# Two more token pairs in the half form of the state space stage

## The chip, the cores and the metric

The kernel runs on one core of one Trainium2 chip. Its time is the device time of one execution in microseconds (us). The core has five engines that work side by side, each through its own list of instructions in order: TensorE (PE in the profile, with its weight loads as PEld), VectorE (DVE), ScalarE (ACT), GpSimd (POOL) and SyncE (SP), which here only issues transfers (DMAs). They wait for each other by semaphores.

## The reference

A state space layer is followed by a two-layer network. Per batch, head and chunk the first one computes, with L the decay between two positions and `state` carried from chunk to chunk:

```
CB = einsum('bhin,bhjn->bhij', Cc, Bc);  M = CB * L
y  = einsum('bhij,bhjd->bhid', M, xc) + einsum('bhin,bhnd->bhid', Cc, state) * decay_to_i
state = decay_full * state + sum_j Bc * xc * decay_from_j
h = x @ w_in;  g = max(h, 0) + alpha * min(h, 0);  out = g @ w_out
```

There are 4 batches, 8 heads, 768 positions, 32 values per head and 16 state rows; the result, 3072 tokens of 256 values, goes through w_in (256 x 2048) and w_out (2048 x 256). All is float32. The chunk in the kernel is 128 positions (the result does not depend on it).

## The kernel before

**Tokens.** The 3072 tokens are 24 chunks of 128, worked in 12 pairs (0 to 11) of two chunks; a batch has 3 pairs, so pairs 2, 5, 8 and 11 end one. Two pairs fill one block of 512 tokens, of which the network handles one at a time; there are 6 blocks.

**First block.** `first_two` handles pairs 0 and 1. The loop over `f` (16 slices of the hidden layer) then runs the network on block 0 by `hidden(0, f)` (two products into a PSUM tile `hp`, then the activation on ScalarE, L1098, and on VectorE, L1099) and `output(f - 4)`, and among them the conversion of the weights (`convert_a`, `convert_b`: L273 and L286 on ScalarE, L278 and L330 on GpSimd, L296 and L308 on VectorE), pairs 2 and 3, and the loads of pairs 3 and 4 (`load_pair`, at f = 5 and 10). There are two `hp` tiles, so a product into one waits until VectorE has read what was in it before. At f = 14 VectorE also runs the scans over the rows of `a` of batches 2 and 3 (L437 to L483), and GpSimd makes `bn` (B times the decay to the end, `pair_loads`, L533) for pair 4.

**Later blocks.** `quad(g, z, after, third)` is a quarter of the hidden layer for block g: products `first` (L1241) into `ss` and `hp` tiles, the activations (`prelu`, L1224 and L1226), and sums of results on GpSimd (L1288, L1298). Its calls `after(j)` place everything else by hand: `product` (L1216), the last `output` steps of block 0 (L1142), weight sums on GpSimd (`weight_sums`, L1171) and the steps of the pairs (table `steps`). The second product of a quad, into `Y` with weights `s1`, takes the token sum `t1` that GpSimd makes in `token_sums` (L1183); `Y` of the first quad is the `hp` tile of `hidden(0, 15)`.

**A pair** (`pair(gp)`, a generator): `added` makes the state update (L629), `states` applies it (L642), `sm` masks the state on GpSimd (L645), B and C are turned so that positions lie along the free axis, `scan_half` makes the decays on VectorE from rows loaded in `abc`, `spread_c` and `c_decayed` make `cz` (ScalarE, L679) and `cd` (GpSimd, L682), `products_bc` makes C·B into `gram` tiles (two `ss`, two `hp`), VectorE multiplies them with the decays (L753), and the products with x and with the state give `y` (L797 and L805), which ScalarE copies to `xT`.

**Full and half form.** Pairs 2 to 5 use the full form: products over 128 positions and scans of 256 columns (L567). Pairs 6 to 11 (`gp >= HALF`) use the half form: the two halves of a chunk of 128 positions are handled as 64 each, on the two halves of the partitions, so that the part of the 128x128 square above the diagonal that is zero is not computed. The decay rows are 192 columns (`SQ`) rather than 256 (scans at L561), the products are L618, L731, L779 and L787, and two copies each of `cd` (ScalarE, L690) and of the state (GpSimd, L692) move them to the other half of the partitions (`moved`). The loads are 64 partitions at a time (L146, L154), 17 DMAs for a pair.

**Turning.** Pairs 5 to 11 load B and C so that VectorE turns them in one instruction (`turn_bc`, L574), with the first two decay scans behind it; pairs 2 to 4 are turned by TensorE (four transposes, L669) and a copy on ScalarE (L672).

**Constants.** `m5_bank` is a PSUM bank whose right half holds the identity that the scans read; `halve_identity` rewrites its lower partitions for the half form. `scratch["z", i]` are the decay rows in DRAM, from which `abc` is loaded; `prt` holds the decays to the end, turned by `rows_turn`.

Of the kernel before, what the change touches and what calls it, by code (L numbers as in the profile page):

```python
# [9 lines left out]
F32 = mybir.dt.float32  # L10
# [12 lines left out]
def kernel(  # L23
# [25 lines left out]
    nc = tc.nc  # L49
# [4 lines left out]
    batch, H, S, D = x.shape  # L54
# [22 lines left out]
    WQ = 256  # L77
    HQ = Q // 2
    SQ = Q + HQ
    HALF = NP // 2  # L80
    assert H * N == P and HD == d_model and KC == 2 and R == CPB == 6
    assert NCH % GC == 0 and GT == 512 and NF % 8 == 0 and d_model <= WQ

# [65 lines left out]
    def load_spread(gp, b, c):  # L149

        for w, t in enumerate(loads["p", gp][1] if gp >= HALF else ()):
            rows = scratch["z", b // 2].rearrange("(b h c) t -> b c h t", b=2, h=H)
            for k in range(2):
                nc.sync.dma_start(  # L154
                    out=t[HQ * k : HQ * (k + 1), : 4 * SQ].rearrange("p (h t) -> p h t", h=4),
                    in_=rows[b % 2, c + k, 4 * w : 4 * w + 4].unsqueeze(0)
                    .to_broadcast([HQ, 4, SQ]))
        for k, t in enumerate(loads["p", gp][1] if gp < HALF else ()):
            rows = scratch["z", b // 2].rearrange("(b h c) t -> b c h t", b=2, h=H)[b % 2, c + k]
            nc.sync.dma_start(out=t.rearrange("p (h t) -> p h t", h=H),  # L160
                              in_=rows.unsqueeze(0).to_broadcast([P, H, Q]))
            yield
# [7 lines left out]
    def load_pair(gp, decays=True, parted=False):  # L170


        b, c = divmod(2 * gp, CPB)
        turned = gp > GC
        nat = ldx.tile([P, 3, 2, H * N], F32, name="nat")
        xt = ldx.tile([P, 2, HD], F32, name="xt")

        ap = ldx.tile([P, 2 * Q], F32, name="ap")
        if gp == 0:
            load_a(ap, b, c)  # L180
        elif gp > NB:
            load_products(gp, ap)
        if gp == 0:
            load_rows(0, nc.scalar)
        abc = []
        if gp >= HALF:
            load_tokens(nat[:, 0], B[b], c * Q)
        def load_bc(k):
            ts = slice((c + k) * Q, (c + k + 1) * Q)
            for i, src in enumerate((B,) if turned else (B, C)):  # L190
                eng = nc.scalar if gp == 0 and i else nc.sync
                eng.dma_start(out=nat[:, i, k].rearrange("p (h n) -> p h n", h=H),  # L192
                              in_=src[b, :, ts, :].rearrange("h p n -> p h n"))

        def load_x(k):
            ts = slice((c + k) * Q, (c + k + 1) * Q)
            nc.sync.dma_start(out=xt[:, k].rearrange("p (h d) -> p h d", h=H),  # L197
                              in_=x[b, :, ts, :].rearrange("h p d -> p h d"))

        for k in range((1 if parted else 2) if gp < HALF else 0):  # L200
            load_bc(k)
            if gp >= NB:
                load_x(k)
        for k in range(2 if gp < NB else 0):
            load_x(k)
        if gp == 0:
            nc.scalar.dma_start(out=al_n, in_=moe_alpha.rearrange("(k p) -> k p", p=P))
            loads["a", 1] = prep.tile([P, 2 * Q], F32, name="a1")
            load_a(loads["a", 1], b, c + 2)
        for i, src in enumerate((B, C) if turned else ()):  # L210


            for e in range(2):
                first = src[b, e : e + 1, c * Q : (c + 2) * Q, :]
                nc.sync.dma_start(out=nat[:, 1 + e, i],
                                  in_=bass.AP(tensor=first.tensor, offset=first.offset,
                                              ap=[[2 * S * N, P // 32], [8 * N, 32], [1, 8 * N]]))
        for k in range(2 if gp >= NB else 0):
            abc.append(lda.tile([P, H * Q], F32, name="abc"))
        loads["p", gp] = nat, abc, xt, ap  # L220
        if gp >= HALF:
            load_tokens(xt, x[b], c * Q)
        if decays:
            for part in load_spread(gp, b, c):
                pass
        return lambda: load_bc(1), lambda: load_x(1)
# [193 lines left out]

    def halve_identity():

        for s in range(2):
            nc.scalar.copy(
                out=ident_p[0][HQ:].rearrange("p (a s t) -> p s a t", a=2, s=2)[:, s],
                in_=ident[HQ:, HQ * (1 - s) : HQ * (2 - s)].unsqueeze(1).to_broadcast([HQ, 2, HQ]))
# [45 lines left out]
    def rows_out(i):  # L472


        if i == 0:
            scratch["z", 0] = dr.tile([RW, Q], F32, name="z0")
            nc.sync.dma_start(out=scratch["z", 0], in_=held.pop("z"))
            return
        d0 = held.pop(i)[:, :SQ]
        rpf = prep.tile([RW, Q], F32, name="rpf")  # L480
        nc.vector.tensor_tensor_scan(out=rpf, data0=d0[:, :Q], data1=zeros[:RW], initial=1.0,
                                     op0=ALU.mult, op1=ALU.add)
        nc.vector.memset(d0[:, :1], 0.0)  # L483
        for key, t in (("z", d0), ("pf", rpf)):
            scratch[key, i] = dr.tile([RW, t.shape[1]], F32, name=f"{key}{i}")
            nc.sync.dma_start(out=scratch[key, i], in_=t)

    def rows_short(r):

# [31 lines left out]
    def pair_loads(gp):  # L521

        b, c = divmod(2 * gp, CPB)
        nat, abc, xt, ap = loads["p", gp]

        bn = work.tile([P, 2, H * N], F32, name="bn")
        i, bi = divmod(b, 2)
        if gp >= HALF:
            pj = prt[i].rearrange("p (j b m h) -> p j b m h", j=2, b=2, h=H)[:, :, bi, c // 2]
        else:  # L530
            pj = (prt[i if gp >= NB else "short"]
                  .rearrange("p (b h c) -> p b c h", b=2, h=H)[:, bi, c : c + 2])
        nc.gpsimd.tensor_tensor(  # L533
            out=bn.rearrange("p k (h n) -> p k h n", h=H),
            in0=nat[:, 0].rearrange("p k (h n) -> p k h n", h=H),
            in1=pj.unsqueeze(3).to_broadcast([P, 2, H, N]), op=ALU.mult)
        return bn
# [43 lines left out]
    def pair(gp):  # L581
# [24 lines left out]

        shifted = one.tile([P, 2, P], F32, name="shifted") if half else None

        def added_halves(banks):


            dps = [t[:, : 4 * D].rearrange("p (k m) -> p k m", k=2) for t in banks]
            for j in range(2):
                for r in range(4):
                    rs, hs = slice(32 * r, 32 * r + 32), slice(2 * r * D, 2 * (r + 1) * D)
                    for k in range(nk):
                        ks = slice(HQ * k, HQ * (k + 1))
                        nc.tensor.matmul(dps[k][rs, k], bn[ks, j, rs], xt[ks, j, hs],  # L618
                                         start=False, stop=j == 1,
                                         tile_position=(HQ * k, 32 * r),  # L620
                                         skip_group_check=True)
            return dps
# [30 lines left out]
        if fine:  # L653
            bn = bns.pop(gp) if gp in bns else pair_loads(gp)
            if half:
                dps = added_halves(beside.pop(gp))
            else:
                dps = added(beside.pop(gp) if gp in beside else ss_tile()[:, : 2 * Q])
            yield
            states(dps)  # L660
            yield
# [92 lines left out]
            if i == 1:  # L754
                yield
        if fine and gp + 1 < NP:
            if gp + 1 == HALF:
                halve_identity()
                halved.append(True)
            turn_bc(gp + 1)  # L760
        yield

# [691 lines left out]
    for f in range(FIRST, NF):  # L1454
        if f in (5, 10):
            load_pair(3 + f // 10)
        if f == 5:
            load_rows(1)
        hidden(0, f)
        for part in range(2):  # L1460
            if part:
                if f <= 10:
                    ssm(2)
                if f >= 9:
                    ssm(3)
            for i in CONVERTED.get((f, part), ()):
                if isinstance(i, str):
                    convert_a(*pieces[int(i)])
                else:
                    convert_next(first=False)  # L1470
        if f == 14:
            bns[4] = pair_loads(4)
            rows_clamp(1)
            held["pr"] = rows_scan(1)
            rows_out(1)
        if f == 8:
            bns[3] = pair_loads(3)
        output(f - FIRST)
        if f in in_steps:
            weight_sums(wi, in_sums, 0, in_steps[f])  # L1480
    early[0] = None
    beside[GC] = m5_bank[0][:, : 2 * Q]
    token_sums(1)
    ssm(2 * GC // 2, 4)

# [94 lines left out]
```

## Time and profile before

| | |
|---|---|
| time, median of 3 runs (lowest to highest) | 355.99 us (355.82 to 357.87) |
| span of the profiled execution | 355.9 us |
| TensorE clock granted | 1.00 in all stages |
| busy: PE, PEld, DVE, ACT, POOL | 349.3, 284.4, 235.8, 171.8, 204.4 us |
| DMA | 30.24 MB, 105581 packets |

The profile's page gives busy times and the chain of work that ended last; its trace can be asked for the instructions of one engine in order of time (the timeline: start, length, engine, line, operation, tiles, count, and in brackets the idle time before with what ended it), for one line's instructions, and for the busy time in stretches of the span. All times are from the start of the span. Neighbouring instructions overlap by some hundredths of a microsecond.

### The profile page before, as it was taken

Reading aid. Unit: us, or ns where it says so; the run is one execution under the profiler, and the core shown is the slowest. Engines: PE = TensorE matmul, PEld = TensorE weight load, DVE = VectorE, ACT = ScalarE, POOL = GpSimd, SP = SyncE. Lnnn points to the kernel's source line nnn. Section 1 sums busy time; section 2 is a strip of 40 time slices with the busy share of each in tenths; the row PEclk is TensorE's granted clock in tenths of the full one; section 3 lists DMA queues with packets and bytes.
Section 4 is the critical chain, followed back from the end, with each engine's and each line's share of the span. In section 5 each row is a group of like instructions: output and inputs, shape, how many; then the busy total and the mean of one; then the engine's idle time right before and its main releaser. Section 6 shows DMA issues by size and latency. Waiting matters only on the chain.

```text
span 355.9 us, 7778 instructions
## 1 busy us (share of the span) xinstructions
PE 349.3 (98%) x2985; PEld 284.4 (80%) x2985; DVE 235.8 (66%) x482; ACT 171.8 (48%) x391; POOL 204.4 (57%) x228
## 2 busy tenths in 40 slices
PE   8899999999999999999999999999999999999996
PEld 4576665578788888888888888888888888888885
DVE  6876986998748756847747856757856633643363
ACT  3477576535355346345345445345445344443431
POOL 6776568589939855725646626637526535434520
PEclk9999999999999999999999999999999999999999
DMA  7899989607345403503423423422001001001102
GB/s 138 182 202 270 329 174 279 148 17 159 106 83 128 102 3 75 104 2 77 78 57 74 86 51 71 85 55 65 11 2 31 0 2 29 2 1 31 31 0 59
DMA packets 105581, 30.24 MB, mean 85 GB/s; under 512 B 79896, under 2 KB 101448, under 8 KB 105544
## 3 DMA queue, kind: packets, MB, share of 16 engines
q1 hardware_dynamic: 103048, 29.43, 36.3%
q10 hardware_dynamic: 2496, 0.32, 0.6%
q8 instruction: 23, 0.38, 0.5%
q14 instruction: 14, 0.11, 0.1%
HBM read 26.32 MB, written 3.42 MB: 84 GB/s over the span
## 4 chain that ended last, share of the span: by engine, by line
PE 89%; SPq 4%; DMA 3%; DVE 2%; ACT 1%; POOL 1%; issue 0%; DVEq 0%; ACTq 0%
PE bank L1216 33%; PE hp L1241 29%; PE bank L1142 6%; PE ss L1241 6%; PE hp L1095 3%; DMA raw<-in_moe_w_in_dram 2%; SPq L192 2%; PE ss L787 1%; PE ss L731 1%; PE hp L1110 1%; PE bank L1209 1%; PE ss L805 1%; PE ss L779 1%; DMA xt<-in_x_dram 1%; SPq L197 1%; PE ss L742 1%
## 5 line engine op out<-in xcount | busy, mean ns | idle before, releaser
L1298 POOL TENSOR_TENSOR gt<-gt 128x512 f32<-128x512 f32 x58 | 74.2, 1279 | 21.1 <-DVE gt L1226 16.3
L1216 PE MATMUL bank<-gt,w_out 128*128 128x256 f32 x320 | 83.5, 381 | 0.0
L1216 PEld LDWEIGHTS bank<-gt,w_out 128*128 128x128 f32 x320 | 60.1, 190 | 9.2 <-issue 1.0
L1288 POOL TENSOR_TENSOR gt<-gt 128x512 f32<-128x512 f32 x20 | 25.4, 1269 | 62.5 <-DVE gt L1226 49.7
L1226 DVE SCALAR_TENSOR_TENSOR gt<-hp,s_mul,gt 128x256 f32<-128x256 f32 x96 | 42.0, 479 | 29.1 <-ACT gt L1224 26.8
L1224 ACT ACTIVATE gt<-hp,s_alpha 128x256 f32<-128x256 f32 x96 | 40.3, 471 | 34.5 <-PE hp L1241 31.4
L1216 PE MATMUL bank<-gt,ws 128*128 128x256 f32 x224 | 55.9, 379 | 0.0
L1216 PEld LDWEIGHTS bank<-gt,ws 128*128 128x128 f32 x224 | 42.3, 190 | 5.6
L1241 PE MATMUL hp<-xs,w_in 128*128 128x256 f32 x160 | 41.9, 384 | 0.0
L1241 PE MATMUL hp<-xs,ws 128*128 128x256 f32 x160 | 41.1, 380 | 0.0
L1267 DVE TENSOR_TENSOR hp<-hp,u 128x512 f32<-128x512 f32 x20 | 14.0, 700 | 35.2 <-ACT u L1265 35.2
L1241 PEld LDWEIGHTS hp<-xs,ws 128*128 128x128 f32 x160 | 30.3, 190 | 4.3 <-POOL xs L1183 0.2
L1241 PEld LDWEIGHTS hp<-xs,w_in 128*128 128x128 f32 x160 | 29.7, 190 | 4.5
L1142 PE MATMUL bank<-w_out,gt 128*128 128x256 f32 x128 | 31.1, 385 | 0.4 <-POOL w_out L330 0.4
L1142 PEld LDWEIGHTS bank<-w_out,gt 128*128 128x128 f32 x128 | 23.6, 190 | 7.2 <-issue 2.9
L1241 PE MATMUL ss<-xT,w_in 128*128 128x256 f32 x96 | 24.6, 379 | 0.0
L645 POOL TENSOR_TENSOR sm<-state,bmask 128x256 f32<-128x256 f32 (+1 forms) x10 | 6.2, 620 | 29.0 <-DVE state L642 29.0
L1095 PE MATMUL hp<-xT,w_in 128*128 128x512 f32 x48 | 22.8, 596 | 0.0
L561 DVE TENSOR_TENSOR_SCAN dec<-abc,bank 128x192 f32<-128x192 f32 x48 | 22.7, 522 | 0.0
L1256 ACT COPY m<-hp 128x512 f32<-128x512 f32 x8 | 4.7, 586 | 35.7 <-PE hp L1241 35.7
L1265 ACT COPY u<-hp 128x512 f32<-128x512 f32 x20 | 11.7, 585 | 19.4 <-PE hp L1241 19.4
L1226 DVE SCALAR_TENSOR_TENSOR gt<-c,s_mul,gt 128x256 f32<-128x256 f32 x40 | 20.6, 555 | 0.0
(232 smaller groups left out, 608.2 us busy)
## 6 DMA issues: line engine op xcount, KB each, us to landing
abc<-z SPq DMA_DIRECT2D x24, 192.0 KB
raw<-in_moe_w_in_dram SPq DMA_DIRECT2D x8, 512.0 KB
raw<-in_moe_w_out_dram SPq DMA_DIRECT2D x8, 512.0 KB
abc<-z SPq DMA_DIRECT2D x8, 512.0 KB
out_dram<-o_sb SPq DMA_DIRECT2D x32, 64.0 KB
nat<-in_B_dram SPq DMA_DIRECT2D x26, 64.0 KB
xt<-in_x_dram SPq DMA_DIRECT2D x12, 128.0 KB
xt<-in_x_dram SPq DMA_DIRECT2D x24, 64.0 KB
```

Of the source, the lines that this page charges most:

```text
L192: eng.dma_start(out=nat[:, i, k].rearrange("p (h n) -> p h n", h=H), in_=src[b, :, ts, :].rearrange("h p n -> p h n"))
L561: nc.vector.tensor_tensor_scan(out=dv[:, o : o + SQ], data0=abc[k][:, s : s + SQ], data1=ident_p[0][:, :SQ], initial=0.0, op0=ALU.mult, op ...
L1095: nc.tensor.matmul(hp, w_in[:, k, f * P : (f + 1) * P], xts[g][:, k], start=(k == 0), stop=(k == KC - 1))
L1142: nc.tensor.matmul(pos[0][t // 2][:, t % 2], gt[:, t * Q : (t + 1) * Q], w_out[:, f], start=(f == 0 and t % 2 == 0), stop=(f == NF - 1), s ...
L1216: nc.tensor.matmul(ms[g][i][:, h], w, blocks[g, z][n][:, p], start=(q == 0 and h == 0), stop=(q == NQ - 1), skip_group_check=True)
L1224: nc.scalar.mul(o[:, p], h[:, p], s_alpha[:, fs[p]])
L1226: nc.vector.scalar_tensor_tensor(out=o[:, p], in0=h[:, p], scalar=s_mul[:, fs[p]], in1=o[:, p], op0=ALU.mult, op1=ALU.max)
L1241: nc.tensor.matmul(to[:, p], w(2 * z + p), b, start=start and p == 0, stop=True, skip_group_check=True)
L1265: nc.scalar.copy(out=u2, in_=A)
L1267: nc.vector.tensor_tensor(out=Y, in0=Y, in1=u2, op=ALU.add)
L1288: nc.gpsimd.tensor_tensor(out=tc_, in0=g22, in1=g12, op=ALU.subtract)
L1298: eng.tensor_tensor(out=o, in0=x0, in1=x1, op=ALU.subtract)
```

## The change

`HALF` becomes 4, so that pairs 4 and 5 take the half form, and `turned` holds for pair 4 too: its B and C are loaded for VectorE and turned there, in a call `turn_bc(4)` at f = 14, ahead of the row scans. What the half form needs for batches 0 and 1 is added: `rows_repeated` (f = 6) extends the decay rows to 192 columns on GpSimd and writes them to DRAM, `rows_halved` (f = 12) rearranges `prt` of batch 1 by four GpSimd copies, and `halve_identity` moves from the end of pair 5 to f = 13. The state update of pair 4 goes to `m5_bank` and to half of an `ss` tile.

```diff
-    HALF = NP // 2
+    HALF = GC
...
-            rows = scratch["z", b // 2].rearrange("(b h c) t -> b c h t", b=2, h=H)
+            rows = scratch["zs", b // 2].rearrange("(b h c) t -> b c h t", b=2, h=H)
...
-        turned = gp > GC
+        turned = gp >= GC
...
+    def rows_repeated():
+        d0 = held.pop(0)
+        nc.gpsimd.tensor_copy(out=d0[:, Q + 1 :], in_=d0[:, HQ + 1 : Q])
+        nc.gpsimd.memset(d0[:, :1], 0.0)
+        scratch["zs", 0] = dr.tile([RW, SQ], F32, name="zs0")
+        nc.sync.dma_start(out=scratch["zs", 0], in_=d0)
+
+    def rows_halved():
+        t = prep.tile([P, RW], F32, name="prth")
+        for v in range(2):
+            for j in range(2):
+                nc.gpsimd.tensor_copy(
+                    out=t[HQ * v : HQ * (v + 1)]
+                    .rearrange("p (j b m h) -> p j b m h", j=2, b=2, h=H)[:, j],
+                    in_=prt[0][HQ * j : HQ * (j + 1)]
+                    .rearrange("p (b h m k) -> p k b m h", b=2, h=H, k=2)[:, v])
+        prt["halves"] = t
...
-            pj = prt[i].rearrange("p (j b m h) -> p j b m h", j=2, b=2, h=H)[:, :, bi, c // 2]
+            pj = prt[i if i else "halves"].rearrange(
+                "p (j b m h) -> p j b m h", j=2, b=2, h=H)[:, :, bi, c // 2]
...
-                                         start=False, stop=j == 1,
+                                         start=fresh and j == 0, stop=j == 1,
...
-                dps = added_halves(beside.pop(gp))
+                dps = added_halves(beside.pop(gp), gp == HALF)
...
-            if gp + 1 == HALF:
-                halve_identity()
-                halved.append(True)
             turn_bc(gp + 1)
...
+        if f == 6:
+            rows_repeated()
+        if f == 12:
+            rows_halved()
+        if f == 13:
+            halve_identity()
         if f == 14:
             bns[4] = pair_loads(4)
+            turn_bc(4)
             rows_clamp(1)
             held["pr"] = rows_scan(1)
             rows_out(1)
...
-    beside[GC] = m5_bank[0][:, : 2 * Q]
+    beside[GC] = [m5_bank[0][:, : 2 * Q], ss_tile()[:, 2 * Q :]]
```

More of the change, by code (lines that the diff above doesn't have):

```diff
@@ L421, in halve_identity @@
     def halve_identity():
+        halved.append(True)
         for s in range(2):
@@ L483, in rows_out @@
         nc.vector.memset(d0[:, :1], 0.0)
-        for key, t in (("z", d0), ("pf", rpf)):
+        for key, t in (("zs", d0), ("pf", rpf)):
             scratch[key, i] = dr.tile([RW, t.shape[1]], F32, name=f"{key}{i}")
             nc.sync.dma_start(out=scratch[key, i], in_=t)
+    def rows_repeated():
[14 more added lines that the diff above has]
+        prt["halves"] = t
     def rows_short(r):
@@ L607, in pair, with added_halves @@
         shifted = one.tile([P, 2, P], F32, name="shifted") if half else None
-        def added_halves(banks):
+        def added_halves(banks, fresh=False):
             dps = [t[:, : 4 * D].rearrange("p (k m) -> p k m", k=2) for t in banks]
```

## The prediction

> **What bounds the kernel now.** First the page's busy times and its chain of waits:
>
> ```profile
> PE 349.3 (98%) x2985; PEld 284.4 (80%) x2985; DVE 235.8 (66%) x482; ACT 171.8 (48%) x391; POOL 204.4 (57%) x228
> PE 89%; SPq 4%; DMA 3%; DVE 2%; ACT 1%; POOL 1%; issue 0%; DVEq 0%; ACTq 0%
> ```
>
> TensorE carries 89% of the chain; a microsecond that it no longer works, or newly waits, counts in full. Next the busy time in stretches (columns: stretch, its length, busy PE, PEld, DVE, ACT, POOL with instruction counts, granted clock, DMA share, GB/s), where the change is made:
>
> ```profile
> 60.00:70.00 10.00, 10.00 (x48) 6.23 (x47) 9.52 (x17) 6.08 (x11) 5.87 (x7) 1.00 0.74 151
> 70.00:80.00 10.00, 10.00 (x98) 6.78 (x97) 9.28 (x18) 3.06 (x6) 8.19 (x9) 1.00 0.06 15
> ```
>
> TensorE is full, but VectorE has only 1.2 us in 20 free. So the third view is the order of VectorE, TensorE and GpSimd at the hand-over from the first block to the quads:
>
> ```profile
> 74.42 0.69 DVE L308 SCALAR_TENSOR_TENSOR wr<-wt,wr 128x512 uint32<-128x512 uint32 x1 [0.51 <-POOL wt L278]
> 75.39 1.42 DVE L467 TENSOR_TENSOR_SCAN pr<-r,ends 96x128 f32<-96x128 f32 x1
> 77.56 0.75 DVE L1099 SCALAR_TENSOR_TENSOR gt<-hp,s_mul,gt 128x512 f32<-128x512 f32 x1
> 82.92 0.70 DVE L1267 TENSOR_TENSOR hp<-hp,u 128x512 f32<-128x512 f32 x1 [0.62 <-ACT u L1265]
> ```
> ```profile
> 77.63 0.43 PE L629 MATMUL bank<-xt,bn 128*32 128x64 f32 x16
> 77.99 0.65 PE L669 MATMUL ss<-ident,nat 128*128 128x128 f32 x4
> 78.48 1.03 PE L1241 MATMUL ss<-xT,w_in 128*128 128x256 f32 x4
> 79.35 0.47 PE L1241 MATMUL hp<-xs,ws 128*128 128x256 f32 x1
> ```
> ```profile
> 78.55 0.73 POOL L1183 TENSOR_TENSOR xs<-xT 128x256 f32<-128x256 f32 x1
> ```
>
> The 79.35 product is the first quad's Y. It needs t1 (GpSimd, 79.28) and the hp tile that the activation of f = 15 frees at 78.31 (77.56 + 0.75). That is 1.04 us of slack, and turn_bc(4) is put ahead of that activation on VectorE.
>
> **What TensorE saves.** Pair 5 is full, pair 6 half, so the slots are read from one to the next. C·B: 118.47 to 119.55 is 1.08 us, 146.11 to 146.95 is 0.84; 0.24 saved per pair. y: 124.93 to 126.54 is 1.61, 152.33 to 153.66 is 1.33; 0.28 saved. The state update: 0.36 full (77.63 to 77.99), 0.40 half (153.66 to 154.06), so pair 4 loses 0.04; pair 5 ends a batch and has one state only, 0.23 full (98.86 to 99.09) against 0.33 in pair 8 (slot 179.46 to 181.12, less 1.33), so 0.10 lost. Pair 4's transposes, 77.99 to 78.48, save 0.49. All is on the path: 2 x 0.52 + 0.49 - 0.14 = 1.4 us, if nothing else becomes late.
>
> **First wait, at Y.** VectorE gains L574 and two L561 scans before the row scans. Both stand in pair 5's own next-pair step:
>
> ```profile
> 122.07 1.11 DVE L574 STREAM_TRANSPOSE bc<-nat 128x512 f32<-128x512 f32 x1
> 123.04 0.93 DVE L561 TENSOR_TENSOR_SCAN dec<-abc,bank 128x192 f32<-128x192 f32 x2
> ```
>
> From 122.07 to 123.97, less an overlap of 0.05: 1.85 us. Queued behind them are the row scans and the activation of f = 15. Four GpSimd copies (f = 12) come in front of the weight sum at 70.19; the nearest row, L692 (64x128), is 0.286 us, a 64x48 copy somewhat less: 0.9 us together, of which 0.70 us is GpSimd's idle time before 72.36. The remainder, and how VectorE's L308 at 70.64 (1.58 us beside that sum, 0.69 elsewhere) meets the moved sum, pass by L330 and L278 to the L308 at 74.42: 0.15 to 0.75 late, I take 0.35. So the f = 15 activation ends at 78.31 + 1.85 + 0.35 = 80.5, and Y starts there instead of 79.35: 1.2 us later (0.8 to 1.7), although TensorE is ready at 78.9. The wait of some 1.6 us swallows the saved transposes. t1 (79.6) is earlier. Then VectorE recovers: state 0.6 and four scans of 0.46 end at 83.0, and L1267 waits for u, 1.2 us later than before.
>
> [...]
>
> **After Y** the savings left are 0.24 + 0.28 - 0.10 + 0.24 + 0.28 = 0.94 us: 1.2 - 0.94 = +0.26 so far.
>
> **Second wait, at pair 5's C·B.** The half form puts `moved` on ScalarE: two copies of cd behind cz, which wait for GpSimd's cd. Behind them stand the activations of the same quad:
>
> ```profile
> 111.77 0.90 ACT L679 ACTIVATE cz<-bc,par 128x256 f32<-128x256 f32 x2
> 113.69 0.84 ACT L1224 ACTIVATE gt<-hp,s_alpha 128x256 f32<-128x256 f32 x2 [1.01 <-issue]
> 140.60 0.61 ACT L690 COPY shifted<-cd 64x128 f32<-64x128 f32 x2
> ```
> ```profile
> 113.82 0.73 POOL L682 TENSOR_TENSOR cd<-bc,ap 128x256 f32<-128x256 f32 x1
> 115.75 1.45 POOL L1171 TENSOR_TENSOR w_out<-w_out 128x512 f32<-128x512 f32 x1
> ```
> ```profile
> 117.40 0.86 DVE L1226 SCALAR_TENSOR_TENSOR gt<-hp,s_mul,gt 128x256 f32<-128x256 f32 x2
> ```
>
> In pair 6 cd is done before ScalarE is. In pair 5 GpSimd still has weight sums in front of it and ends cd at 114.55, so the copies run 114.55 to 115.15 and the activation of 113.69 starts 1.46 us later. The last activation of the quad frees the hp tile at 118.26; C·B starts at 118.47 and its products for r = 2 go into that tile: slack 0.2 us. At most 1.46 - 0.2 = 1.25 us are lost; at least none, if VectorE, whose L1226 pair at 115.41 took 2.07 us beside GpSimd's sums and 0.87 at 143.19 beside none, meets less of them. I take 0.8: GpSimd ends its sums 0.57 us later (two copies of 0.286), so most of the contention stays.
>
> [...]
>
> In pair 4 the copies wait for cd until 85.5, and the activation behind them starts at 86.8 at the earliest (85.68 + 1.2): nothing lost.
>
> **What lies in the shadow.** rows_repeated is a copy of 96x63 and a memset (0.1 us, L455), 0.4 us at most, in front of the L278 of 42.01; L308 uses that at 43.74, so the cover is 1.1 us. Its DMA (72 KB) moves three weight loads by half a microsecond, and these are converted 10 us later. halve_identity (2 x 0.26 us) falls into ScalarE's idle 1.15 us before 70.98 and leaves a gap at 122. Two copies of 0.286 on GpSimd in pair 4 take its 0.76 us before 88.62. VectorE's shorter scans and multiplications (0.55 for 0.68) take nothing off the path.
>
> **Loads.** Pair 4's load is 17 DMAs for 9. SP stalls behind the weight loads until 60.7 as before; by then three are out, and 14 at 0.62 us (pair 6: four L146 in 2.70) end at 69.3. Before, the last went out by 64.15 and traffic was over at 68.5, so I expect arrival near 72; turn_bc(4) wants them at 75.4. Pair 5's loads start 2.2 us later, behind the row DMAs, and end near 91.5; they are wanted at 94, with 1.6 us of idle VectorE behind.
>
> **Forecast.** +0.26 + 0.8 = +1.06: 356.98 on the profiled 355.92, which stands 0.07 below the median; on 355.99 it is 357.0. With the bounds (first wait -0.4 or +0.5, second -0.8 or +0.45) the case spans 355.9 to 358.0. A change under 1% (352.4 to 359.6) is what I call the same.
>
> **Rivals.**
> 1. *Only the first wait*: cd comes earlier, since GpSimd can use its idle time before pair 5's sums. 355.99 + 0.26 = 356.2. For: GpSimd idles 2.06 us at 101.7. Against: that idle time waits for VectorE, not for work.
> 2. *The saving arrives*: VectorE is no gate, its 1.58, 1.11 and 1.42 us rows shrink to 0.69, 0.42 and 0.42 (L467's other run) as GpSimd's work moves. That is 2.6 us against 2.2 added, and the result is 355.99 - 1.4 = 354.6. Against: GpSimd works in that stretch as much as before.
> 3. *Slower: pair 4's loads come late.* VectorE stands at turn_bc(4), and the activation of f = 15, hence Y, stands behind it. It decides from an arrival after 75.4; every further microsecond counts in full, so arrival at 77 to 79 adds 1.6 to 3.6: 358.6 to 360.6, beyond 1% only past 78. For: 14 issues in a row behind a saturated stretch. Against: 3 us of margin.
> 4. *The edit does not take*: the instruction order of the changed kernel shows the 64-row products in pairs 4 and 5 and no L669 in pair 4; ruled out.
>
> **Chances.** Forecast 0.55, rival 1 0.18, rival 2 0.12, rival 3 0.10, anything else 0.05. Range 354.9 to 358.9: it leaves out the lower half of rival 2, most of rival 3 and the rest. Faster by over 1% would need 3.6 us where 1.4 are to be had: 0.02. Slower by over 1%, half of rival 3 and of the rest: 0.08. The same: 0.90.
>
> **What would show it.** In the changed profile: C·B and y of pairs 4 and 5 at 0.84 and 1.33 us; the transposes gone; a wait of TensorE at the first quad's Y, put down to VectorE's L1099, with Y near 80.5; the shifted copies on ScalarE ending idle time on GpSimd's cd near 115, and a second wait of TensorE at pair 5's C·B. Wrong would be a TensorE without idle time between 77 and 80, a VectorE that stands before L574 for a DMA, or a new wait elsewhere.

## The result, and the profile after

The changed kernel takes 361.26 us, median of 6 runs (359.33 to 362.33). Beside it the kernel before took 356.71 us (355.82 to 357.87, 6 runs). The ratio is 1.0123, with a 95% interval of 1.010 to 1.0145: slower by 1.0 to 1.45%, and outside the forecast range. The times of the changed kernel stand in two groups. Two runs, with a mean granted clock of 1.000, took 359.33 and 359.37 us; four, with a clock of 0.990 to 0.994, took 361.16 to 362.33 us. So there are two losses to explain: one of nearly 3 us that all runs have, and one of 2 to 3 us more that comes with the clock.

One thing for reading times: in every run that lists both, the time is 1.7 us above the span. The profiled execution of the changed kernel has a span of 360.6 us and took 362.33.

Line numbers have moved: the row activation L1099 is now L1118, the first product L1095 is L1114, L574 is L596, L561 is L583, L1241 is L1260, L1226 is L1245, L682 is L704, L690 is L712, L731 (C·B) is L753; L629 became L640 in the half form.

Of the changed kernel's page, the busy times, the row of the granted clock in 40 slices, and the chain of waits:

```profile
PE 351.6 (98%) x3101; PEld 286.5 (79%) x3101; DVE 233.7 (65%) x483; ACT 172.7 (48%) x394; POOL 207.1 (57%) x238
...
PEclk9999999996999999999999999999999999999999
...
PE 83%; DVE 6%; POOL 4%; SPq 3%; issue 1%; DMA 1%; ACT 1%; DVEq 0%; POOLq 0%; ACTq 0%
```

The saved products are not to be seen in the sum: TensorE is busy for 2.3 us longer (349.3 before). The clock row shows why, a 6 in the slice that begins at 81 us. And 10% of the chain now lies on VectorE and GpSimd, where it was 3%. Next the stretches of 2 us around that slice (length, busy PE, PEld, DVE, ACT and POOL, granted clock, DMA share, GB/s):

```profile
76.00:78.00 2.00, 1.37 (x37) 1.01 (x36) 2.00 (x4) 0.00 (x0) 2.00 (x4) 1.00 0.00 0
78.00:80.00 2.00, 0.50 (x3) 0.10 (x1) 1.92 (x6) 0.57 (x1) 1.92 (x4) 1.00 0.00 0
80.00:82.00 2.00, 1.29 (x3) 1.14 (x4) 1.90 (x6) 0.00 (x0) 1.76 (x4) 0.51 0.22 62
82.00:84.00 2.00, 2.00 (x6) 1.55 (x6) 0.94 (x3) 0.58 (x1) 1.92 (x2) 0.50 0.49 94
84.00:86.00 2.00, 2.00 (x7) 1.55 (x6) 0.00 (x0) 0.00 (x0) 1.80 (x5) 0.50 0.41 41
86.00:88.00 2.00, 2.00 (x9) 1.69 (x8) 1.10 (x3) 1.10 (x3) 2.00 (x2) 0.78 0.24 73
```

TensorE works 0.50 us of the 2 before 80, while VectorE and GpSimd are full. Then the clock is 0.50 from 80.05 to 86.88 (an estimate from the mean clocks of the stretches), and TensorE, busy from 80.71 on, has six or seven products at work in 2 us where there are eleven at full clock (kernel before, 82 to 84 us). The timeline of TensorE in that stretch names the waits:

```profile
76.87 0.28 PE L640 MATMUL bank<-xt,bn 64*32 64x64 f32 x2 [0.63 <-POOL bn L555]
...
80.71 2.04 PE L1260 MATMUL hp<-xs,ws 128*128 128x256 f32 x4 [2.21 <-DVE gt L1118]
82.55 1.91 PE L1161 MATMUL bank<-w_out,gt 128*128 128x256 f32 x4
```

80.71 is the Y of the forecast, put down to VectorE's activation of f = 15 as foreseen, but after 2.21 us of waiting and not 1.6, and with a second wait of 0.63 us, for GpSimd's `bn`, just ahead. That 80.71 is so near to the 80.5 of the forecast is chance: this execution runs 1.46 us ahead of the one of before at that point (see below). Each group of four products then takes 1.9 to 2.0 us instead of 1.03. VectorE in the same stretch:

```profile
74.10 0.69 DVE L308 SCALAR_TENSOR_TENSOR wr<-wt,wr 128x512 uint32<-128x512 uint32 x1 [1.85 <-POOL wt L278]
74.71 1.12 DVE L596 STREAM_TRANSPOSE bc<-nat 128x512 f32<-128x512 f32 x1
75.67 0.94 DVE L583 TENSOR_TENSOR_SCAN dec<-abc,bank 128x192 f32<-128x192 f32 x2
...
76.80 1.27 DVE L459 TENSOR_SCALAR r<-rows 96x63 f32<-96x63 f32 x1
...
78.10 0.87 DVE L468 TENSOR_TENSOR_SCAN pr<-r,ends 96x128 f32<-96x128 f32 x1
78.90 0.88 DVE L482 TENSOR_TENSOR_SCAN rpf<-r,zeros 96x128 f32<-96x128 f32 x1
79.82 0.75 DVE L1118 SCALAR_TENSOR_TENSOR gt<-hp,s_mul,gt 128x512 f32<-128x512 f32 x1
```

And GpSimd, which VectorE waits for at 74.10 and works beside at 76.80:

```profile
68.72 1.89 POOL L502 COPY prth<-prt 64x48 f32<-64x48 f32 x4
...
76.75 1.27 POOL L1190 TENSOR_TENSOR w_in<-w_in 128x512 f32<-128x512 f32 x1
77.97 0.73 POOL L1202 TENSOR_TENSOR xs<-xT 128x256 f32<-128x256 f32 x1
78.78 0.72 POOL L1202 TENSOR_TENSOR xs<-xT,xs 128x256 f32<-128x256 f32 x1
```

In the kernel before, the clamp that is now L459 (there L458) started ahead of GpSimd's next instruction and not behind it:

```profile
75.17 0.18 DVE L458 TENSOR_SCALAR r<-rows 96x63 f32<-96x63 f32 x1
```
```profile
75.26 1.26 POOL L330 TENSOR_TENSOR w_out<-wr,wg 128x512 uint32<-128x512 uint32 x1 [0.87 <-DVE wr L308]
```

Executions differ before this point, mostly in waits for converted weights before 46 us (TensorE waits 0.85 us at 14.11 and 0.44 at 45.84 before; after, 0.51 at 13.74 and nothing at the second place), so places are best compared from the start of the first product of f = 15 (74.09 before, 72.63 after). From there, the activation of f = 15 ends after 4.22 us before (78.31) and after 7.94 now (80.57): 3.72 us later. L308 stands 1.14 us later in the same measure.

The second wait, at pair 5's C·B, in the timelines of GpSimd, ScalarE and TensorE:

```profile
115.33 1.28 POOL L1190 TENSOR_TENSOR ws<-w_out 128x512 f32<-128x512 f32 x1
116.69 1.28 POOL L1190 TENSOR_TENSOR ws<-ws,w_out 128x512 f32<-128x512 f32 x1
117.93 0.73 POOL L704 TENSOR_TENSOR cd<-bc,ap 128x256 f32<-128x256 f32 x1
```
```profile
118.69 0.60 ACT L712 COPY shifted<-cd 64x128 f32<-64x128 f32 x2 [1.93 <-POOL cd L704]
```
```profile
122.55 0.45 PE L753 MATMUL ss<-cz,bc 32*64 32x256 f32 x4
...
123.45 0.43 PE L753 MATMUL hp<-cz,bc 32*64 32x256 f32 x2 [0.23 <-DVE gt L1245]
...
124.25 1.13 PE L1235 MATMUL bank<-gt,w_out 128*128 128x256 f32 x4
```

GpSimd's two weight sums stand ahead of `cd`, ScalarE's copies stand until 118.69 for it, and C·B takes 1.70 us (122.55 to 124.25) instead of 0.84. The loss is 0.86 us; the bracket of 0.23 counts only the moment in which nothing at all of C·B ran.

The whole balance can be read from three places: f = 15, Y, and the last group of 36 products. The step from Y to the last group is 263.84 us before and 266.93 after.

### The profile page after: what moved, and what is told of

It is laid out like the page before. It is cut to its first block, busy times and chain, and to the rows that moved or that the text cites. A ratio compares the mean times of both kernels' runs of the same rounds, so it can differ in the third digit from the quotient of the medians.

```text
span 360.6 us, 8043 instructions
## 1 busy us (share of the span) xinstructions
PE 351.6 (98%) x3101; PEld 286.5 (79%) x3101; DVE 233.7 (65%) x483; ACT 172.7 (48%) x394; POOL 207.1 (57%) x238
## 4 chain that ended last, share of the span: by engine, by line
PE 83%; DVE 6%; POOL 4%; SPq 3%; issue 1%; DMA 1%; ACT 1%; DVEq 0%; POOLq 0%; ACTq 0%
PE bank L1235 31%; PE hp L1260 28%; PE bank L1161 5%; PE ss L1260 5%; PE hp L1114 3%; PE ss L806 2%; SPq L192 2%; PE ss L753 1%; DVE dec L589 1%; PE ss L798 1%; PE hp L1129 1%; POOL gt L1317 1%; POOL ws L1190 1%; DVE gt L1245 1%; PE bank L1228 1%
## 5 line engine op out<-in xcount | busy, mean ns | idle before, releaser
L1245 DVE SCALAR_TENSOR_TENSOR gt<-hp,s_mul,gt 128x256 f32<-128x256 f32 x96 | 42.0, 479 | 31.0 <-ACT gt L1243 27.2
L1260 PE MATMUL hp<-xs,ws 128*128 128x256 f32 x160 | 43.0, 393 | 2.2 <-DVE gt L1118 2.2
L1260 PE MATMUL hp<-xs,w_in 128*128 128x256 f32 x160 | 41.9, 384 | 0.0
L1260 PEld LDWEIGHTS hp<-xs,ws 128*128 128x128 f32 x160 | 31.4, 197 | 7.0 <-POOL xs L1202 2.6
L1260 PEld LDWEIGHTS hp<-xs,w_in 128*128 128x128 f32 x160 | 29.7, 190 | 4.5
L1161 PE MATMUL bank<-w_out,gt 128*128 128x256 f32 x128 | 32.0, 392 | 0.0
L583 DVE TENSOR_TENSOR_SCAN dec<-abc,bank 128x192 f32<-128x192 f32 x64 | 30.3, 525 | 0.0
L1260 PE MATMUL ss<-xT,w_in 128*128 128x256 f32 x96 | 25.2, 386 | 0.0
L1114 PE MATMUL hp<-xT,w_in 128*128 128x512 f32 x48 | 22.7, 595 | 0.0
L1294 DVE TENSOR_TENSOR c<-hp,m 128x512 f32<-128x512 f32 x20 | 13.8, 692 | 11.0 <-PE hp L1260 11.0
```

What stands on the lines that cost most here:

```text
L583: nc.vector.tensor_tensor_scan(out=dv[:, o : o + SQ], data0=abc[k][:, s : s + SQ], data1=ident_p[0][:, :SQ], initial=0.0, op0=ALU.mult, op ...
L1114: nc.tensor.matmul(hp, w_in[:, k, f * P : (f + 1) * P], xts[g][:, k], start=(k == 0), stop=(k == KC - 1))
L1161: nc.tensor.matmul(pos[0][t // 2][:, t % 2], gt[:, t * Q : (t + 1) * Q], w_out[:, f], start=(f == 0 and t % 2 == 0), stop=(f == NF - 1), s ...
L1245: nc.vector.scalar_tensor_tensor(out=o[:, p], in0=h[:, p], scalar=s_mul[:, fs[p]], in1=o[:, p], op0=ALU.mult, op1=ALU.max)
L1260: nc.tensor.matmul(to[:, p], w(2 * z + p), b, start=start and p == 0, stop=True, skip_group_check=True)
L1294: nc.vector.tensor_tensor(out=c22, in0=A, in1=m5, op=ALU.add)
```

## Experiments

The theory: (a) VectorE's turn and scans, and GpSimd's four copies, both delay the activation of f = 15, and with it Y; (b) TensorE's idle time there makes the clock fall; (c) the second wait eats most of what is saved. Rivals for each stand with the runs. In the table, "Y" is the distance from the start of the first product of f = 15 to that of Y, and the next column that from Y to the last group, both in the profiled execution.

| kernel | time, median (us) | against before, 95% | Y | Y to last group | clock of the runs |
|---|---|---|---|---|---|
| before | 356.3 to 356.7 | | 5.26 | 263.84 | 0.994 to 1.000 |
| after | 361.26 | 1.010 to 1.0145 | 8.08 | 266.93 | 0.990 to 1.000 |
| copies earlier | 359.74 | 1.0056 to 1.0124 | 6.95 | 263.88 | 0.993 to 1.000 |
| turn later and copies earlier | 360.46 | 1.0071 to 1.0145 | 7.72 | 263.80 | 0.995 to 1.000 |
| turn later | 362.48 | 1.013 to 1.022 | 10.14 | 265.43 | 0.991 to 0.995 |
| wait filled, first attempt | 363.88 | 1.0176 to 1.0262 | 10.91 | 264.97 | 0.991 to 0.995 |
| pair 5 alone | 359.46 | 1.0031 to 1.0086 | 6.36 | 264.46 | 0.999 to 1.000 |
| wait filled | 359.51 | 1.0049 to 1.0101 | 8.07 | 263.88 | 0.998 to 1.000 |
| before, two scans more | 357.97 | 1.0012 to 1.0058 | 6.53 | 263.83 | 0.994 to 1.000 |
| before, four scans more | 360.75 | 1.0068 to 1.0141 | 8.12 | 263.84 | 0.994 to 1.000 |
| scans behind | 356.77 | 0.9985 to 1.0016 | 5.23 | 264.04 | 0.995 to 1.000 |
| scans behind, sums earlier | 356.43 | 0.9982 to 1.0017 | 5.23 | 263.20 | 0.995 to 1.000 |
| the same again | 356.31 | 0.9971 to 1.0015 | 5.23 | 263.20 | 0.999 to 1.000 |

**Products of constants in the wait (first attempt).**

```diff
+            if (g, z) == (1, 0):
+                keep_warm(spare_ss, 4)
         first(Y, lambda q: s1[:, q], t1, True)
...
-    beside[GC] = [m5_bank[0][:, : 2 * Q], ss_tile()[:, 2 * Q :]]
+    spare_ss = ss_tile()
+    beside[GC] = [m5_bank[0][:, : 2 * Q], spare_ss[:, 2 * Q :]]
```

> The changed kernel with four products of constants (128x256, some 0.43 us each) put on TensorE between the first quad's Z and Y, where it stood idle for 2.2 us; they write a free half of an ss tile. Theory 1 (the idle time halves the clock): the granted clock stays at 1.00 from 80 to 90 us, Y still waits for VectorE's L1118 until about the same time, and all runs lie near the changed kernel's best, 359.3 us, spread under 1 us. Theory 2 (the clock falls for another cause, a DMA or load on the chip): the clock still falls to 0.5 in some runs, and times spread from 359 to 362 us as before.

Measured: 363.88 us (362.87 to 365.11), ratio 1.0176 to 1.0262, clock 0.991 to 0.995. TensorE's timeline:

```profile
80.88 2.55 PE L338 MATMUL ss<-const-float32-1.0 128*128 128x256 f32 x8 [2.68 <-DVE state L664]
```

The products waited themselves: the other half of that `ss` tile holds pair 4's state update, and VectorE reads it only after the activation of f = 15, from 80.55 to 80.83. So nothing was filled, and the four products came on top. The run does not show what filling does; its own wait of 2.68 us left all four runs with a lower clock.

**The turn later, the copies earlier, and both.** First the turn alone:

```diff
             bns[4] = pair_loads(4)
-            turn_bc(4)
...
     early[0] = None
+    turn_bc(4)
```

> The changed kernel with turn_bc(4) moved behind the loop over f, so on VectorE behind the row scans and the activation of f = 15. Theory 1 (what stands in front of that activation holds Y): the activation ends 2 us earlier, Y waits for GpSimd's t1 at most, TensorE idles under 1 us there, the clock stays at 1.00, and the time is 356.5 + 1.0 = 357.5 us (356.8 to 358.2). Theory 3 (GpSimd's four copies at f = 12, 1.9 us, are the main cause, through bn, t1 and the conversion): Y still starts 2 us late, the time is over 359 us.

Measured: 362.48 us (361.61 to 364.35), ratio 1.013 to 1.022. Counted from f = 15, its activation came 2.6 us earlier than in the changed kernel (at 77.40), as meant, but TensorE waited all the same, one step before:

```profile
80.21 0.39 PE L640 MATMUL bank<-xt,bn 64*32 64x64 f32 x2 [3.81 <-DVE dec L583]
```

Pair 4's state update writes the left half of `m5_bank`, and the scans now queued ahead of it read the identity in its right half. The wait had only moved, and grown: the time is 4 us and more above what I expected, and the clock fell in all four runs. Next the copies alone:

```diff
+        if f == 11:
+            rows_halved()
         hidden(0, f)
...
-        if f == 12:
-            rows_halved()
```

> The changed kernel with rows_halved moved from f = 12 to the start of f = 11, into a wait of GpSimd of 2.6 us. Theory 1: VectorE's L308 comes 0.8 us earlier, but the turn and the scans still stand before the activation of f = 15: Y some 2 us later than before, time 358.0 to 359.0 us, the clock falling in fewer runs. Theory 3: Y is back within 0.7 us, time under 357.5 us.

Measured: 359.74 us (359.02 to 360.24), ratio 1.0056 to 1.0124, above the 358.0 to 359.0 expected: the clock fell in three of the four runs, and the fourth took 359.02. L308 waits 0.50 us again, as before the change, and there is no wait for `bn`. Y comes 6.95 us after f = 15, so 1.69 of the 2.82 us remain: that is the share of turn and scans. GpSimd's and VectorE's timelines of this run:

```profile
61.73 1.17 POOL L502 COPY prth<-prt 64x48 f32<-64x48 f32 x4
...
76.49 1.27 POOL L1190 TENSOR_TENSOR w_in<-w_in 128x512 f32<-128x512 f32 x1
```
```profile
76.53 1.27 DVE L459 TENSOR_SCALAR r<-rows 96x63 f32<-96x63 f32 x1
```

The same four copies take 1.17 us here and 1.89 at f = 12. And VectorE's small clamp L459, 0.18 us in the kernel before, lasts as long as GpSimd's 128x512 sum that started just ahead of it. Both at once:

> Both moves. Theory 1 with the copies as a second part: Y within 0.3 us of its old place, so that half of the transposes' 0.49 us and the 0.8 us saved behind Y remain, against 0.9 us of wait at pair 5's C·B: 356.0 to 357.0 us where before is 356.5. If either theory alone held, it would equal e2 (theory 1 alone) or e3 (theory 3 alone) within 0.3 us.

Measured: 360.46 us (359.34 to 361.05), ratio 1.0071 to 1.0145: better than the turn alone, but 3.5 us and more above what I expected, with the state update still waiting 2.64 us for the scans.

**Pair 5 alone in the half form.** Pair 4 stays as it was, and no B and C are turned ahead of the row scans; the copies stay at f = 12.

```diff
-    HALF = GC
+    HALF = GC + 1
...
-            turn_bc(4)
```

> Only pair 5 runs in the half form; pair 4 keeps the form, the transposes and the state update of the kernel before, the identity is halved behind pair 4's scans, and GpSimd's row copies stay at f=6 and f=12. Theory (the first wait belongs to pair 4's part: scans and turn ahead of f=15's activation; the second wait to pair 5's): Y waits about 0.5 us at most (GpSimd's copies alone), the clock is 1.00, and pair 5's C.B product waits about 0.9 us; time = before + 0.9 - 0.5 (pair 5's C.B and y) + 0.3 to 0.8 for the copies: 356.8 to 357.8 beside a before of 356.4. Rival (the copies by themselves bring the wait and the clock's fall): 359 or more.

Measured: 359.46 us (357.91 to 359.91), ratio 1.0031 to 1.0086, all clocks 0.999 or 1.000. That is more than I expected. VectorE and TensorE:

```profile
75.42 0.69 DVE L308 SCALAR_TENSOR_TENSOR wr<-wt,wr 128x512 uint32<-128x512 uint32 x1 [1.85 <-POOL wt L278]
```
```profile
78.29 0.43 PE L651 MATMUL bank<-xt,bn 128*32 128x64 f32 x16 [0.72 <-POOL bn L555]
```

The copies by themselves keep L308 waiting for 1.85 us and TensorE for 0.72 at `bn`, and Y is 1.10 us late. With the 1.69 of the run before that makes 2.79, against 2.82 for the whole change: the two add up, and nothing else delays Y by more than some hundredths.

**Both waits taken away.** The copies at f = 11, and the turn behind pair 4's state update; `dec` is then picked up in `pair` after the state update.

```diff
-            turn_bc(4)
...
-    ssm(2 * GC // 2, 4)
+    ssm(4, 2)
+    turn_bc(4)
+    ssm(4, 2)
```

> GpSimd's four copies move from f=12 to the start of f=11, and VectorE's turn of pair 4's B and C with its two scans moves behind pair 4's state update, so that neither the scans nor the state update stand ahead of the activation of f=15, and TensorE's state update into the left half of the identity's bank no longer waits for scans that read its right half. Theory (the whole loss is the first wait and the slow clock that it sets off; the second wait, about 0.86 us, stays): Y waits under 0.5 us, the granted clock is 1.00 in every run, and the time is that of the kernel before less 0.7 us of saved TensorE work plus 0.86 us: within 0.7 us of it, 355.8 to 357.2 beside a before of 356.4. Rival (the half form costs more than it saves elsewhere, whatever the first wait): still 2 us or more above the kernel before.

Measured: 356.77 us (356.04 to 358.72, 12 runs) beside 356.56 (24 runs), ratio 0.9985 to 1.0016. Y is at 5.23, as in the kernel before. The second wait is still there. In the next kernel two weight sums leave GpSimd's queue ahead of pair 5's `cd`:

```diff
-                 (1, 4): ((wi, in_sums, 4, 2),), (1, 8): ((wi, in_sums, 4, 3),),
-                 (2, 2): ((wqt, out_sums, 4, 0),), (2, 4): ((wqt, out_sums, 4, 1),),
+                 (1, 4): ((wi, in_sums, 4, 2),), (1, 8): ((wi, in_sums, 4, 3), (wqt, out_sums, 4, 0)),
+                 (1, 10): ((wqt, out_sums, 4, 1),),
```

> As the run before (scans behind), and two of GpSimd's weight sums of the third quad are done in the second quad, where GpSimd waits (after places 8 and 10), so that pair 5's decayed C is not queued behind them. Theory: the second wait is only GpSimd's queue, so the 0.86 us ahead of pair 5's C.B product go down to under 0.2 us and the time is 0.6 to 0.9 us below the run with the scans behind alone: 355.0 to 356.4, at or below the kernel before. Rival: ScalarE or VectorE is next late at the same place (the shifted copies beside VectorE's own work), and under 0.3 us is won.

Measured: 356.43 us (355.45 to 357.78), ratio 0.9982 to 1.0017. ScalarE's and TensorE's timelines:

```profile
112.03 0.60 ACT L712 COPY shifted<-cd 64x128 f32<-64x128 f32 x2
```
```profile
117.80 0.45 PE L753 MATMUL ss<-cz,bc 32*64 32x256 f32 x4
...
118.42 0.29 PE L753 MATMUL hp<-cz,bc 32*64 32x128 f32 x4
118.64 1.13 PE L1235 MATMUL bank<-gt,w_out 128*128 128x256 f32 x4
```

ScalarE no longer waits, C·B takes 0.84 us, and from f = 15 to the last group the execution is 0.84 us shorter than the one with the scans behind alone. So the second wait was GpSimd's queue and nothing more. The medians moved by 0.34 us only, so the kernel was run once more:

> The version with the scans behind the state update and the two weight sums in the second quad, unchanged, in another set of runs beside the kernel before, because its profiled execution was 0.67 us shorter than that of before from f=15 on while the medians lay only 0.13 us apart. Theory (the saving of TensorE's work arrives once both waits are gone): 0.3 to 1.0 us below the kernel before, ratio 0.997 to 0.999. Rival (something in the part before f=15 gives it back): ratio 1.000 or above.

Measured: 356.31 us (355.26 to 357.58) beside 356.48 (24 runs), ratio 0.9971 to 1.0015. From f = 15 on, both profiled executions of this version are 0.67 us shorter than that of before (268.43 against 269.10), in the same hundredths. But where f = 15 starts varies from 72.14 to 74.09 us among the profiled executions of all these kernels, and this drowns it. It is the best version of the study; that it is faster than the kernel before is not shown.

**The wait filled, now in a free bank.** The changed kernel, with four products of constants where TensorE stands idle.

```diff
+        if (g, z) == (1, 0):
+            keep_warm(bank(2), 4)
         first(Y, lambda q: s1[:, q], t1, True)
```

> The changed kernel with four products of constants (128x256, about 0.43 us each) between the first quad's first and second product, into a bank that nothing else uses at that time, so that TensorE works through most of the 2.2 us in which it stood idle; nothing else is changed, and the second product can't start earlier. Theory (the idle time itself lets the clock fall, and costs another 2 to 3 us): granted clock 1.00 in all runs, all of them near the 359.3 us that the changed kernel has where its clock is 1.00, so a median of 359.0 to 359.8 with a spread under 1 us. Rival (the clock falls for another reason, as VectorE's and GpSimd's load at that time): the clock still falls in some runs and the times stay at 361 to 362.

Measured: 359.51 us (358.71 to 360.36), ratio 1.0049 to 1.0101, clock 0.998 or more in all four runs; they spread over 1.65 us where under 1 was expected. TensorE:

```profile
78.93 1.90 PE L338 MATMUL bank<-const-float32-1.0 128*128 128x256 f32 x8
81.15 1.10 PE L1260 MATMUL hp<-xs,ws 128*128 128x256 f32 x4 [0.32 <-DVE gt L1118]
82.09 1.03 PE L1161 MATMUL bank<-w_out,gt 128*128 128x256 f32 x4
```

Y is as late as in the changed kernel (8.07 against 8.08), VectorE and GpSimd do the same work, and the products behind it run at full clock (1.00 in each stretch of 2 us from 78 to 86). From f = 15 to the last group this takes 271.95 us against 275.01: 3.06 us are the clock's in the profiled execution. In the medians the four useless products take 1.75 us off (361.26, beside a before of 356.71, to 359.51, beside 356.56); these are two sets of runs, of 6 and 4, whose intervals against before just touch. They end where the two undisturbed runs of the changed kernel stand, 359.33 and 359.37.

**The wait without the change.** The kernel before, with VectorE's reversed row scan repeated ahead of the activation of f = 15; the added results are not used.

```diff
+            for _ in range(2):
+                rows_scan(1)
             held["pr"] = rows_scan(1)
```

> The kernel before, with VectorE's reversed scan of the rows of a (96x128, 1.42 us in the kernel before, with a 0.06 us memset) done three times instead of once at f=14, ahead of the activation of f=15; the first two results are not used. Nothing of the change is in it. The activation of f=15 comes 2.9 to 3.0 us later, and had some 0.9 us of slack at Y. Theory (VectorE's time ahead of that activation by itself brings the wait at Y, and about 2 us of idle TensorE sometimes lets the clock fall): Y waits about 2.0 us; runs whose clock stays are 2 us above the kernel before, the others 4 to 5 us, the median 358.3 to 361.5. Rival for the wait (it needs GpSimd's copies or the half form): under 0.5 us above the kernel before. Rival for the clock (it falls only beside something that the half form adds): all runs at clock 0.998 or more and a median of 358.3 to 359.

Measured: 357.97 us (356.97 to 359.74, 10 runs), ratio 1.0012 to 1.0058. The added scans took 0.56 and 1.19 us, not 1.42 each, so Y waits 1.10 us and is 1.27 late. Nine of ten runs keep a clock of 0.999 or more; the tenth has 0.994 and is the longest. With four more scans:

> The same with five scans instead of one: 5.9 us more on VectorE, so that Y waits about 5 us. Theory (idle time lets the clock fall, the longer the surer): the clock falls in every run, for about as long after the wait as in the changed kernel (6.5 us at half speed, about 3 us of time), so every run is 7.5 to 8.5 us above the kernel before: 364 to 365. Rival (the fall's length goes with the idle time, or its chance does not grow with it): runs at 361 to 362 with the clock kept, or above 366.

Measured: 360.75 us (358.91 to 361.56, 5 runs), ratio 1.0068 to 1.0141. TensorE:

```profile
80.62 1.10 PE L1241 MATMUL hp<-xs,ws 128*128 128x256 f32 x4 [2.69 <-DVE gt L1099]
```

Again a shorter wait than the 5 us aimed at, so that neither the 364 to 365 us nor a fall in every run came, and by chance the very lateness of the changed kernel (Y at 8.12). Two runs with a clock of 1.000 took 358.91 and 359.24 us, three with 0.994 or 0.995 took 360.75 to 361.56. So a late activation of f = 15 alone, with nothing of the half form in the kernel, gives both the loss and the two groups of times of the changed kernel. Whether the fall becomes certain with a longer wait is open: with 3.81 us (the turn later) it came in four of four runs, too few to tell.

## Why the prediction was wrong

**The step that failed** is the first wait. Its place, its cause and the engine named were right; it was taken as 1.2 us at Y (0.8 to 1.7) and is 2.82, because two of its terms were too small:
- *The copies.* "0.9 us together", at somewhat less than 0.286 us each, and L308 0.35 us late. At f = 11 each of the four does take 0.25 to 0.26 us, 1.17 from the first's start to the last's end. At f = 12, beside VectorE's conversions and activation, they take 0.26 to 0.76, 1.89 together, and L308 was 1.14 late. The row was the right one; that it came from a place where only scans of VectorE ran beside it (139.86 us) was not weighed. GpSimd then also ended `bn` 1.02 us late, counted from f = 15, for which the prediction had no term.
- *The turn and the scans.* 1.85 us was right for themselves (1.81 from 74.71 to the row section's start at 76.52). But the row section behind them was taken as moved unchanged, and it grew from 2.5 to 3.3 us (L438 to L1118: 75.03 to 77.56 before, 76.52 to 79.82 after), because L459 now starts just behind GpSimd's sum and takes 1.09 us more, while the first scan, 1.42 us beside GpSimd's L330 before, takes 0.55 less. 1.14 + 1.81 + 0.77 = 3.72 us, where 0.35 + 1.85 = 2.2 was forecast. Less the 1.04 us of slack this is 2.68; Y was 2.82 late.

The ends of these rows go with GpSimd's: L459 ends 0.05 us after the sum, and each of the two scans of the row section ends 0.27 to 0.29 us after the GpSimd instruction during which it starts, in the kernel before and after.

L459 takes 1.27 us beside a 1.27 us sum of GpSimd in three kernels (changed, first attempt, copies earlier), and 0.18 us in the kernel before, where it starts 0.09 us ahead of GpSimd's instruction. What ties the two engines was not shown.

**The step that was missing** is the clock. The prediction priced idle TensorE at its own length. Here 2.2 us of it, after 0.63 shortly before, took the clock down in four of six runs. In the profiled one it stood at 0.50 for 6.8 us, and that cost 3.06 us, more than the wait itself; between the medians of the runs with and without the fall lie 2.4 us. The clock row of the profile before, 1.00 throughout, could not show it.

**The sum** from f = 15 to the last group: 269.10 before, + 2.82 (Y) + 3.06 (clock) + 0.03 (all the rest) = 275.01, as measured. Forecast: + 1.2 - 0.94 + 0.8 = + 1.06.

**After Y** the forecast was -0.94 of saved work and +0.8 of the second wait, -0.14 together; the run with the filled wait shows +0.04. The second wait was right in cause and size: 0.86 and 0.84, from two kernels. The VectorE pair behind it took 1.58 us beside GpSimd's sums, and the loss did not come near the 1.25 us that the prediction named as its bound. What is saved is a third smaller, 0.64 us, seen alone when both waits are gone. Slot by slot in the changed kernel: 0.25 and 0.24 for the two C·B, 0.24 for pair 5's y, as forecast; but pair 4's y with pair 5's state update saves 0.05 instead of 0.18. The slots come to 0.78, the whole to 0.64. The difference lies in one slot: with both waits gone pair 4's C·B takes 1.10 us, not 0.98 as in the changed kernel (1.23 before); why is open. The kernel with pair 5 alone loses 0.62 us behind Y: 0.59 in pair 5's C·B with its wait, and 0.25 in pair 4's y with pair 5's state update (1.97 us for 1.72, of which 0.13 is the half form of the update), less 0.24 in pair 5's y.

**The saved transposes** were right in that they bring nothing at Y, but not only because VectorE is late: with Y's wait on VectorE gone, Y still stands at 5.23 us after f = 15 (5.26 before), now behind GpSimd's t1, for which TensorE waits 0.17 us (scans behind).

**The base.** Span and time were taken as one, with the profile 0.07 us below the median. The time is 1.7 us above the span, so the profile before, span 355.9, belongs to some 357.6 us and is 1.6 above the median; its f = 15 starts later, at 74.09, than in any other profiled execution here. This did not enter the differences. But the forecast of 357.0 stood on 355.99, the median of three runs, and six runs give 356.71: 0.7 of the 4.3 us between forecast and result are the base.

**The rivals.** Only the first wait: refuted, the second is there. The saving arrives: refuted as the kernel stood, 0.64 of 1.4 us of it shown once both waits are removed. Late loads of pair 4: refuted, VectorE waits for no transfer at L596, and the last of these loads went out by 65.8 us, not 69.3 (the 0.62 us for each was not even what the row quoted for it gives, 0.68). The rival on the slower side was the wrong one; the right one would have been this same wait with its price doubled by the clock. The chances also failed: 0.90 for no change rested on every error in a wait counting once.

## What to carry to other kernels

Where one engine carries the chain and another is full at a hand-over, put new work of the full engine behind the operation that frees the next buffer, and check what the moved work reads: a PSUM bank whose halves have two uses made the writer of one half wait for the readers of the other here (3.81 us with the turn later). Price an operation of GpSimd or VectorE by a row that had the neighbours it will have. And price idle time of TensorE of some 2 us or more twice, as it was paid here, once for itself and once for the clock behind it (2.21 us of wait, then 3.06 us of clock, in the changed kernel).

## What the runs showed of the hardware

- **Idle time and clock.** Waits of TensorE of 1.10 us left the clock alone in 9 of 10 runs; with 1.90 us (copies earlier) it fell in 3 of 4, with 2.21 in 4 of 6, with 2.64 in 2 of 4, with 2.69 in 3 of 5, with 2.68 (first attempt) and 3.81 (turn later) in 4 of 4 each. The wait is that of the profiled execution, the fall read from mean clocks of 0.995 or less, so where it lay is known only in the profiled executions. Without such a wait 1 or none of 12 runs had such a clock, and of the kernel before 1 of 7, 1 of 24 and 1 of 24.
- **How long the clock stays down.** Of three profiled executions with a fall, two show 6.8 us at 0.50 (changed kernel, 80.05 to 86.88; turn later, 79.42 to 86.25) and one 3.4 us, half as much (first attempt, 82.20 to 85.60). The stretches in which it begins and ends, first those of the turn later, then those of the first attempt:

```profile
79.00:80.00 1.00, 0.00 (x0) 0.00 (x0) 0.95 (x3) 0.00 (x0) 0.92 (x3) 0.71 0.21 59
86.00:87.00 1.00, 1.00 (x6) 0.88 (x5) 0.00 (x0) 0.00 (x0) 0.86 (x3) 0.88 0.68 142
```
```profile
82.00:83.00 1.00, 1.00 (x5) 0.80 (x4) 0.62 (x2) 0.00 (x0) 0.92 (x2) 0.60 0.53 134
85.00:86.00 1.00, 1.00 (x5) 0.86 (x4) 0.00 (x0) 0.59 (x1) 0.86 (x3) 0.70 0.25 41
```

  In the first attempt the clock fell 1.3 us after TensorE had gone back to work (80.88), in the other two while it was still waiting. Why some executions of a kernel have a fall and others none, and why one length is half the other, the runs do not show.
- **VectorE beside GpSimd.** A VectorE operation of 0.18 us lasts 1.27 us when it starts just behind a 1.27 us sum of GpSimd, and four small copies of GpSimd take 1.17 us beside VectorE's scans and 1.89 us beside its conversions and activation. The cause was not shown in either case.
- **Halves of a PSUM tile.** Writes of TensorE into one half waited for VectorE's reads of the other, 3.81 us in `m5_bank` (turn later, released by L583) and 2.68 us in an `ss` tile (first attempt, released by L664); no run here tried without that wait.
